# A delta-rule recurrence with a Fourier-mixing block: V's scaling, queries' products and one transposition moved in the order of work

## The chip, the cores and the metric

One core of one Trainium2 chip runs the whole kernel. The metric is the device time of one execution in microseconds (us); lower is better. Three runs of the kernel before took 741.8, 743.04 and 745.75 us, so their median is 743.04 us.

## The reference

Two blocks, one after the other. The first runs over 768 steps in order, for 4 batches and 8 heads with 48 values each:

```python
k_n = k / (np.linalg.norm(k, axis=-1, keepdims=True) + 1e-06)
for t in range(S):
    kt, vt, bt = (k_n[:, :, t], v[:, :, t], beta[:, :, t, None])
    y[:, :, t] = np.einsum('bhd,bhde->bhe', q[:, :, t], state)
    v_old = np.einsum('bhde,bhd->bhe', state, kt)
    state = state + bt[:, :, :, None] * np.einsum('bhd,bhe->bhde', kt, vt - v_old)
```

Each head keeps a 48 x 48 state. A step reads the state with the query and then corrects it with the key. The second block takes the 8 heads side by side as x (4 x 768 x 384):

```python
X = np.fft.fft(np.fft.fft(x, axis=1), axis=2)
u = x + np.real(X)
un = (u - mu) / np.sqrt(var + 1e-06)
return u + np.maximum(un @ w_ch1, 0.0) @ w_ch2
```

Here mu and var are the mean and variance of u over the last axis, and the hidden width is 1536. Everything is float32.

## The kernel before

**Tiles.** A batch of 768 steps is cut into 6 loads of 128 steps, and a load into 2 chunks of 64. Within a chunk, the dependence of steps on each other is a triangular 64 x 64 matrix for each head. Its inverse, applied to the keys and the values, turns 64 steps into a few matrix products. Four loads form a round, whose triangular blocks are inverted together on VectorE: 16 x 16 blocks in `invert16` (rounds 0 to 2), 32 x 32 blocks in `invert` (later rounds).

**One load.** Several generators make a load's parts; each `yield` is a point at which other work can be put between.

- `pre_a` transposes the keys (L320) and forms their Gram matrix on TensorE.
- `pre_q` transposes the queries (`turn`, PSUM to QT by ScalarE at L320), multiplies keys with queries (the product written `pair<-QT,KT` in the profile) and masks the result into LQ on VectorE (L555).
- `pre_m16` finishes the inverse of the 64 x 64 matrix from the 16 x 16 blocks. It takes a product with the part above the blocks (`one<-Z,GU`, copied to ND at L617) and then three more products, a short series: `MT,ND`, whose result is subtracted on VectorE (L645, into Z); `Z,ND`, copied by ScalarE into MT (L647); and `MT,ND` again, added on VectorE (L649, into MT). Then the values V are scaled by the keys' norms (L629, on VectorE for the first 8 loads and on GpSimd for later ones). At last, for batch 0, the load's last products `pair<-MT,K` and `one<-V,MT` give WT and U0.
- `step` does one chunk of the recurrence: a product with the state (`pair<-S,WT`), a subtraction from U on VectorE (L720), a product with the keys (`pair<-U,K`) and an addition into the next state S (L739). For later batches the forms are L698 (V less the product with the state) and L708 (U), and the first state of a batch is a copy (L737).
- `outputs` makes y: `pair<-S,QT` (copied to x at L762) and `pair<-U,LQ` (added to x at L772).

**The second block.** `folds` and `fourier` do the transform with tables; `mlp` normalises (un, L911), transposes on TensorE (the tile `ptr`, copied to unT at L922), and makes the products with w1 (tile `ph`, copied to hT at L936) and w2 (tile `po`). The weights arrive as 64-bit numbers and are converted by `weight`: ScalarE (L285, L277, L278) and VectorE (L286, L288, L292, L295, L299) share the work, with a ring of three or four loads E by DMA. A step's L285 waits until L292 of an earlier step has read the scratch tile that it writes.

**PSUM.** There are three rings with two tiles each: `pair`, `one` and `post` (ph, po and ptr). A new tile of a ring waits until the tile before the last one has been read.

**What sets the order.** Up to the middle of batch 0's second block, the order on TensorE, VectorE, ScalarE and GpSimd is written out by hand, as a list of `advance` and `drain` calls (`tc.manual_schedule(engines=engines)`). There the loop `for g in range(NL - 1)` works on load g's recurrence and, between its pieces, on the inverses of the next two loads: `nm` is the one of load g + 1 and `n2` the one of load g + 2. `fill` adds pieces of round 1's inversion, and `convert` pieces of the weights' conversion. `late` is the output of load g - 1. Then come the lines

```python
        done = 3 + KF
        inv = invert16(2)
    with tc.manual_schedule(engines={mybir.EngineType.PE}):
        drain(nq)
        for g in range(NL, NL + 2):
            period(g, side)
```

and for these two loads of batch 1 only TensorE's order is by hand; a scheduler places the others' instructions. Round 2's inversion begins here: its first piece clears M (L474) and transposes the Gram blocks into A (L475), and its next takes the square root of A's diagonal on ScalarE (nrm, L481), followed by a chain of small VectorE operations (L483 to L508) and 15 steps of a multiplication and an addition (L517, L520), with two more transpositions at the end (L523, L526).

Of the kernel before, what the change touches and what calls it, by code (L numbers as in the profile page):

```python
# [20 lines left out]
RL = 4  # L21
# [43 lines left out]
def kernel(  # L65
# [14 lines left out]
    NL = S // L  # L80
# [84 lines left out]
    def load_v(g, engine=None):  # L165
        if g < NLT:
            Vs[g] = wk.tile([128, 2, 4, D], F32, tag="V", bufs=2, name="V")
            halves(Vs[g], v, g, engine)
# [389 lines left out]
    def pre_m(g):  # L558

        r, li = divmod(g, RL)  # L560
        K, V = Ks[g % 3], Vs.pop(g)
        X = GXs[g // 2][:, li % 2]
# [5 lines left out]
                                op=ALU.mult)  # L568
        nc.gpsimd.tensor_tensor(V.rearrange("p c j d -> p (c j) d"),
                                V.rearrange("p c j d -> p (c j) d"),  # L570
# [27 lines left out]
    def pre_m16(g):  # L598


        r, li = divmod(g, RL)
        K, GU = Ks[g % 3], GXs.pop((g, 16))
        MTd, Md, nT = rounds[r]
        m8 = slice(8 * li, 8 * li + 8)
        tags = ("QT", "LQ") if g < 2 * RL else ("WT", "WT")
        Z = wk.tile([128, 8, 2, W], F32, tag=tags[0], bufs=2, name="Z")
        for e in range(2):
            nc.scalar.activation(Z[:, :, e, :], Md[:, m8, :], ACT.Copy, scale=m_blk[:, e:e + 1])
        if g != 2 * RL:
            yield  # L610
        px = ps_one()
        for m in range(8):
            for hh in range(2):
                mm(px[full[hh], C * m:C * m + C], GU[full[hh], m, :],
                   Z[full[hh], m].rearrange("p b t -> p (b t)"), m == 0)
        ND2 = wk.tile([128, 8, C], F32, tag=tags[1], bufs=2, name="ND")
        nc.scalar.activation(ND2.rearrange("p m t -> p (m t)"), px, ACT.Copy)  # L617
        MT = wk.tile([128, 8, 2, W], F32, tag="MT", bufs=2, name="MT")
        for e in range(2):
            if g == 0:  # L620
                nc.vector.tensor_scalar(MT[:, :, e, :], MTd[:, m8, :], m_blk[:, e:e + 1], None,
                                        op0=ALU.mult)
            else:
                nc.scalar.activation(MT[:, :, e, :], MTd[:, m8, :], ACT.Copy,  # L624
                                     scale=m_blk[:, e:e + 1])

        def scaled_v():
            V = Vs.pop(g)
            (nc.vector if g < 2 * RL else nc.gpsimd).tensor_tensor(  # L629
                V.rearrange("p c j d -> p (c j) d"), V.rearrange("p c j d -> p (c j) d"),  # L630
                nT[:, m8, None].broadcast_to([128, 8, D]), op=ALU.mult)
            return V

        V = None if g else scaled_v()
        flat = "p m b t -> p (m b t)"
        yield
        for i in range(3):
            pz = ps_one()
            src = Z if i == 1 else MT
            for m in range(8):  # L640
                for hh in range(2):
                    mm(pz[full[hh], C * m:C * m + C], ND2[full[hh], m, :],
                       src[full[hh], m].rearrange("p b t -> p (b t)"), m == 0)
            if i == 0:
                nc.vector.tensor_tensor(Z.rearrange(flat), MT.rearrange(flat), pz, op=ALU.subtract)  # L645
            elif i == 1:
                nc.scalar.activation(MT.rearrange(flat), pz, ACT.Copy)  # L647
            else:
                nc.vector.tensor_tensor(MT.rearrange(flat), Z.rearrange(flat), pz, op=ALU.add)  # L649
            if i < 2 or g < 2 * RL:  # L650
                yield
        V = V or scaled_v()
        if g >= NL:
            pre[g] = (K, MT, V)
            yield
            return
        yield
        WT = wk.tile([128, 2, 2, 2, C], F32, tag="WT", bufs=2, name="WT")
        U0 = wk.tile([128, 2, 4, D], F32, tag="U0", bufs=2, name="U0")
        pw = ps_pair()  # L660
        pu = ps_one()
        for c in range(2):
            for j in range(4):
                for hh in range(2):
                    mt = MT[full[hh], 4 * c + j].rearrange("p b t -> p (b t)")
                    jj, jp = divmod(j, 2)
                    o = (2 * c + jj) * C
                    mm(pw[full[jp], hh, o:o + C], K[full[hh], 4 * c + j, :], mt, c == 0 and jj == 0)
                    o = (4 * c + j) * D
                    mm(pu[full[hh], o:o + D], mt, V[full[hh], c, j, :], c == 0 and j == 0)  # L670
        nc.scalar.activation(U0.rearrange("p c j d -> p (c j d)"), pu[:, 0:8 * D], ACT.Copy)
        nc.scalar.activation(WT.rearrange("p h c j t -> p h (c j t)"), pw[:, :, 0:4 * C],
                             ACT.Copy)
        pre[g] = (K, WT)
        Us[g] = U0
        yield
# [291 lines left out]
    def advance(gen, n=1):  # L968
        for _ in range(n):
            if next(gen, "end") == "end":  # L970
                return False
        return True

    def drain(gen):
        for _ in gen:
            pass
# [121 lines left out]
    with tc.manual_schedule(engines=engines):  # L1098
# [4 lines left out]
        qs = [pre_q(g, QT6[:, g], LQ6[:, g]) for g in range(NL)]  # L1103
# [60 lines left out]
        def convert(n):  # L1164
            advance(conv, n)
# [9 lines left out]
        for g in range(NL - 1):  # L1175
            c0, c1 = step(g, 0), step(g, 1)
            nm, n2 = ms[g + 1], ms[g + 2]
            load_k(g + 2)
            load_v(g + 2)
            if g == 0:  # L1180
                advance(c0)
                fill(5)
                advance(nm)
                advance(n2)
                advance(c1)
                fill(5)
                advance(nm)
                advance(n2)
                advance(c1)
                fill(5)  # L1190
                advance(nm)
                advance(n2)
                drain(nm)
                advance(n2)
                drain(qs[1])
                advance(qs[2])
                advance(ms[3])
            else:
                advance(c0)
                if g == 2:  # L1200
                    advance(n2)
                else:
                    fill(5)
                if g > 2:
                    convert(1)
                advance(nm)
                advance(late)
                advance(c0)

                fill(5)  # L1210
                if g == 2:
                    convert(1)
                advance(n2)
                drain(late)
                if g == 4:
                    fold = folds(0)
                    fd = part(fold, 8)
                    advance(keys[0])
                advance(nm)
                advance(c1)  # L1220
                fill(4 if g == 1 else 3)
                if g > 1 and g != 4:
                    convert(2)
                drain(nm)
                advance(n2)
                advance(c1)
                if g == 4:
                    convert(2)
                    advance(n2)
                    drain(qs[g + 1])  # L1230
                    convert(1)
                else:
                    fill(1)
                    if g > 1:
                        convert(1)
                    advance(n2)
                    if g > 1:
                        convert(g - 1)
                    drain(qs[g + 1])
                if g + 2 < NL:  # L1240
                    advance(qs[g + 2])
                if g > 1 and g < 4:
                    advance(ms[g + 3])
            late = outputs(g)
            if g == 1:
                nc.sync.dma_start(out=evt, in_=cn["even"].ap())
                nc.sync.dma_start(out=odt, in_=cn["odd"].ap())
                nc.sync.dma_start(out=dtab, in_=cn["dtab"].ap())
            if g == 2:
                for i in range(2 * RL, 2 * RL + 3):  # L1250
                    load_c(i)
                load_q(NL)
                load_q(NL + 1)

        g = NL - 1
# [12 lines left out]
        late = outputs(g)  # L1268
# [4 lines left out]
        late = None  # L1273
# [36 lines left out]
            drain(m)  # L1310
        done = 3 + KF
        inv = invert16(2)
    with tc.manual_schedule(engines={mybir.EngineType.PE}):
        drain(nq)
        for g in range(NL, NL + 2):
            period(g, side)
# [48 lines left out]
```

## Time and profile before

| | us |
|---|---|
| median of three runs | 743.04 |
| the profiled execution | 743.66 |
| its span in the profile | 741.9 |
| TensorE busy in the span | 689.6 |
| VectorE busy | 377.1 |
| ScalarE busy | 262.5 |
| GpSimd busy | 79.1 |

The profiled execution took 0.62 us more than the median of the runs, and 1.76 us of it lie outside the span. In the time line, each row gives the start and the length in us, the engine, the line of the kernel, the operation, the written tile, the read tiles, the shape and the number of instructions. What stands in brackets is the idle time of the engine just before, and the instruction that ended it. In the table of stretches, each engine has its busy time and its number of instructions; the three numbers at the end are TensorE's granted clock as a share of the full clock, the DMA engines' share and GB/s.

The edited code covers these stretches of the span:

| stretch, us | what runs | TensorE busy, us |
|---|---|---|
| 50 to 115 | batch 0's recurrence, loads 0 to 5 | 52.6 of 65 |
| 115 to 160 | batch 0's transform and first products with w1 | 41.6 of 45 |
| 160 to 170 | between the first products and batch 1 | 5.3 of 10 |
| 170 to 200 | batch 1's first load, round 2's inversion | 28.6 of 30 |

### The profile page before, as it was taken

The numbers are of one execution on the slowest core, as the hardware profiler recorded it, in microseconds if no ns is written. First come the engines' busy times: TensorE is split into PE (matmuls) and PEld (weight loads), VectorE is DVE, ScalarE is ACT, GpSimd is POOL, SyncE is SP. The second block draws the span as 40 slices with busy tenths as digits, with TensorE's granted clock in tenths as the row PEclk, the third lists the DMA queues.
The fourth block names the chain that finished last, engine by engine and source line by source line (L and its number), as shares of the span: only waits on it lengthen the run. The fifth ranks groups of instructions, "written<-read, shape, count | busy, mean of one in ns | idle before, by whom it ended". The sixth has DMA issues, their size and how long they took to land.

```text
span 741.9 us, 23087 instructions
## 1 busy us (share of the span) xinstructions
PE 689.6 (93%) x10176; PEld 529.3 (71%) x10176; DVE 377.1 (51%) x957; ACT 262.5 (35%) x641; POOL 79.1 (11%) x138
## 2 busy tenths in 40 slices
PE   6878789969999978999999999999999999999998
PEld 5667777757667656878768778777677687777684
DVE  5877787798711996170596328288212241600000
ACT  4534774787324212234323243133223121221120
POOL 8000001110000102031101120030112100200000
PEclk8699999988999999999999999999999999999999
DMA  9842452153124211003212211001110000000000
GB/s 153 221 72 43 98 140 87 24 138 99 28 51 83 46 34 28 1 11 72 41 39 50 45 40 28 11 23 37 43 34 13 12 12 5 18 1 21 11 11 21
DMA packets 108791, 36.10 MB, mean 49 GB/s; under 512 B 101873, under 2 KB 105234, under 8 KB 108690
## 3 DMA queue, kind: packets, MB, share of 16 engines
q1 hardware_dynamic: 106866, 33.86, 21.1%
q8 instruction: 80, 1.31, 0.8%
q0 software_dynamic: 640, 0.43, 0.4%
q10 hardware_dynamic: 1184, 0.33, 0.3%
q14 instruction: 21, 0.17, 0.1%
HBM read 29.88 MB, written 4.72 MB: 47 GB/s over the span
## 4 chain that ended last, share of the span: by engine, by line
PE 75%; DVE 15%; ACT 6%; issue 2%; DMA 1%; DVEq 0%; ACTq 0%
PE po L110 24%; PE ph L110 21%; PE one L110 15%; PE pair L110 9%; PE one L113 2%; DVE M L450 1%; DVE tmp L446 1%; PE ptr L113 1%; PE unread L1111 1%; DVE tmp L517 1%; DVE M L520 1%; DMA C<-in_k_dram 1%; DVE Z L645 1%; DVE S L739 1%; DVE w L292 1%
## 5 line engine op out<-in xcount | busy, mean ns | idle before, releaser
L110 PE MATMUL po<-w,hT 128*128 128x384 f32 x576 | 204.8, 495 | 0.0
L110 PE MATMUL ph<-unT,w 128*128 128x256 f32 x828 | 197.2, 390 | 0.0
L110 PEld LDWEIGHTS ph<-unT,w 128*128 128x128 f32 x828 | 155.1, 193 | 23.2
L110 PEld LDWEIGHTS po<-w,hT 128*128 128x128 f32 x576 | 103.5, 190 | 56.4
L936 ACT ACTIVATE hT<-ph 128x256 f32<-128x256 f32 x138 | 52.8, 383 | 144.2 <-PE ph L110 143.3
L951 DVE TENSOR_TENSOR x<-x,po 128x384 f32<-128x384 f32 x24 | 13.2, 551 | 107.0 <-PE po L110 107.0
L739 DVE TENSOR_TENSOR S<-S,pair 128x192 f32<-128x192 f32 x40 | 14.0, 351 | 71.2 <-PE pair L110 71.1
L110 PEld LDWEIGHTS one<-V,MT 64*64 64x64 f32 x768 | 31.1, 143 | 20.0 <-issue 7.7
L882 DVE TENSOR_TENSOR x<-x,one 128x193 f32<-128x193 f32 x24 | 8.5, 355 | 66.5 <-ACT Q L873 66.5
L110 PE MATMUL one<-V,MT 64*64 64x48 f32 x768 | 36.4, 230 | 4.2 <-DVE V L698 2.6
L450 DVE TENSOR_TENSOR M<-M,tmp 128x31 f32<-128x31 f32 (+15 forms) x93 | 34.5, 371 | 3.2
L446 DVE TENSOR_TENSOR tmp<-A,M 128x31 f32<-128x31 f32 (+15 forms) x93 | 34.1, 366 | 2.5
L698 DVE TENSOR_TENSOR V<-V,pair 128x192 f32<-128x192 f32 x33 | 11.5, 349 | 37.6 <-PE pair L110 31.4
L110 PE MATMUL one<-MT,ND 64*64 64x64 f32 x768 | 28.9, 225 | 1.1 <-ACT MT L647 0.7
L110 PEld LDWEIGHTS one<-dtab,F 97*128 97x128 f32 (+1 forms) x192 | 25.1, 191 | 6.4 <-ACT KT L320 1.3
L894 POOL TENSOR_SCALAR rstd<-mv 128x1 f32<-128x1 f32 x24 | 6.6, 276 | 216.4 <-DVE mv L890 216.4
L110 PEld LDWEIGHTS one<-MT,ND 64*64 64x64 f32 x768 | 26.5, 141 | 2.3 <-ACT MT L624 1.1
L320 ACT ACTIVATE QT<-one 128x512 f32<-128x512 f32 x24 | 14.3, 595 | 38.7 <-PE one L113 38.6
L110 PE MATMUL one<-dtab,F 97*128 97x97 f32 (+1 forms) x192 | 26.0, 275 | 0.9 <-ACT KT L320 0.9
L566 POOL TENSOR_TENSOR MT<-A,pack 128x512 f32<-128x512 f32 x12 | 12.8, 1067 | 130.3 <-PE one L110 64.8
L110 PEld LDWEIGHTS pair<-U,K 64*64 64x64 f32 x704 | 15.5, 134 | 15.5 <-issue 13.2
L110 PEld LDWEIGHTS pair<-S,KT 48*64 48x64 f32 x528 | 10.7, 133 | 21.7 <-issue 10.9
(181 smaller groups left out, 1029.4 us busy)
## 6 DMA issues: line engine op xcount, KB each, us to landing
w<-in_moe_w_ch_dram SPq DMA_DIRECT2D x12, 384.0 KB, 7.2
E<-in_moe_w_ch_dram SPq DMA_DIRECT2D x12, 384.0 KB, 3.8
out_dram<-x SPq DMA_DIRECT2D x24, 192.0 KB, 1.9
K<-in_k_dram SPq DMA_DIRECT2D x92, 48.0 KB, 2.3
V<-in_v_dram SPq DMA_DIRECT2D x92, 48.0 KB, 2.3
C<-in_k_dram SPq DMA_DIRECT2D x18, 192.0 KB, 9.5
Q<-in_q_dram SPq DMA_DIRECT2D x18, 192.0 KB, 3.4
w<-in_q_dram SPq DMA_DIRECT2D x6, 192.0 KB, 7.9
```

The costliest lines, as they stand in the source:

```text
L110: nc.tensor.matmul(o, lhsT=lhsT, rhs=rhs, start=start, stop=stop, skip_group_check=True)
L113: nc.tensor.matmul(o, lhsT=src, rhs=ident[0:src.shape[0], 0:src.shape[0]], is_transpose=True, start=start, stop=True, skip_group_check=True)
L292: nc.vector.tensor_tensor(pieces[i - lag][1].rearrange("p c f -> p (c f)"), man0, num0.bitcast(F32), op=ALU.mult)
L320: nc.scalar.activation(dst.rearrange("p h j t -> p (h j t)"), pt, ACT.Copy)
L446: nc.vector.tensor_tensor(t, A[:, j + 1:W, j:j + 1].broadcast_to([128, n, j + 1]), M[:, j:j + 1, 0:j + 1].broadcast_to([128, n, j + 1]), o ...
L450: nc.vector.tensor_tensor(M[:, j + 1:W, 0:j + 1], M[:, j + 1:W, 0:j + 1], t, op=ALU.add)
L566: nc.gpsimd.tensor_tensor(MT, MTd[:, m8, None, :].broadcast_to([128, 8, 2, W]), m_blk[:, None, :, None].broadcast_to([128, 8, 2, W]), op=A ...
L698: nc.vector.tensor_tensor(R4, R4, pw[:, :, 0:2 * D].rearrange("p a (j e) -> p a j e", e=D), op=ALU.subtract)
L739: nc.vector.tensor_tensor(s1v, s0.rearrange("p h j e -> p h (j e)"), pk, op=ALU.add)
L882: nc.vector.tensor_tensor(near, near, pb[:, 0, 0:MH + 1], op=ALU.add)
L936: nc.scalar.activation(hT[:, fc, :], ph, ACT.Relu)
L951: nc.vector.tensor_tensor(x[:, T, :], x[:, T, :], po, op=ALU.add)
```

## The change

Three edits, all to the order of work; every instruction that ran before still runs.

1. In `pre_m16`, V is scaled in the same piece as the third product of the series, ahead of the addition at L649, for the first 8 loads. Before, it was a piece of its own after that addition (load 0 has its own place, which stays).
2. In the loop over batch 0's loads, the queries' products (`drain(qs[g + 1])`, and the next load's transposition `advance(qs[g + 2])`) come ahead of the second product of the series of load g + 2 rather than behind it. In the same loop `advance(late)` comes ahead of `advance(nm)`, so that a load's product `pair<-S,QT` stands ahead of the third product.
3. Round 2's inversion makes its first piece (M cleared, A transposed) at the end of the part whose order is all by hand, behind the first products with w1, rather than where the scheduler places it.

```diff
@@ pre_m16
                     mm(pz[full[hh], C * m:C * m + C], ND2[full[hh], m, :],
                        src[full[hh], m].rearrange("p b t -> p (b t)"), m == 0)
+            if i == 2 and V is None and g < 2 * RL:
+                V = scaled_v()
             if i == 0:
                 nc.vector.tensor_tensor(Z.rearrange(flat), MT.rearrange(flat), pz, op=ALU.subtract)
...
-        V = V or scaled_v()
+        if V is None:
+            V = scaled_v()
@@ loop over batch 0's loads
                 if g > 2:
                     convert(1)
+                advance(late)
                 advance(nm)
-                advance(late)
                 advance(c0)
...
                 if g == 4:
                     convert(2)
+                    drain(qs[g + 1])
                     advance(n2)
-                    drain(qs[g + 1])
                     convert(1)
                 else:
                     fill(1)
                     if g > 1:
                         convert(1)
+                    drain(qs[g + 1])
+                    advance(qs[g + 2])
                     advance(n2)
                     if g > 1:
                         convert(g - 1)
-                    drain(qs[g + 1])
-                if g + 2 < NL:
-                    advance(qs[g + 2])
@@ end of the part by hand
         done = 3 + KF
         inv = invert16(2)
+        advance(inv)
     with tc.manual_schedule(engines={mybir.EngineType.PE}):
```

## The prediction

> **What bounds the kernel now.** I read the page first, then the time lines of the matrix engine (PE), VectorE (DVE) and ScalarE (ACT) around the edited places, the chain of waits over the same stretches, and last PE's clock microsecond by microsecond.
>
> ```profile
> PE 689.6 (93%) x10176; PEld 529.3 (71%) x10176; DVE 377.1 (51%) x957; ACT 262.5 (35%) x641; POOL 79.1 (11%) x138
> ...
> PE   6878789969999978999999999999999999999998
> ...
> PEclk8699999988999999999999999999999999999999
> ```
>
> The 741.9 us are PE's nearly everywhere after slice 10 (185 us). All edited code lies before, in slices 2 to 10, where PE has holes. So the question is which wait ends each hole.
>
> ```profile
> 75.58 0.32 PE L110 MATMUL pair<-MT,K 64*64 64x64 f32 x2 [1.37 <-DVE x L772]
> 76.05 0.25 PE L110 MATMUL one<-V,MT 64*64 64x48 f32 x1
> ...
> 106.21 0.68 PE L110 MATMUL pair<-S,QT 48*64 48x48 f32 x32 [1.08 <-DVE LQ L555]
> ...
> 164.22 0.90 PE L113 MATMUL ptr<-pack,un 128*128 128x128 f32 x3 [4.11 <-ACT hT L936]
> ...
> 176.25 0.45 PE L110 MATMUL pair<-S,KT 48*64 48x48 f32 x16
> ...
> 180.25 0.67 PE L110 MATMUL one<-V,MT 64*64 64x48 f32 x16 [0.76 <-DVE V L698]
> ...
> 197.08 0.69 PE L110 MATMUL pair<-QT,KT 48*64 48x64 f32 x32 [0.67 <-DVE S L739]
> ```
>
> PE waits for DVE at the head of each load's last products (75.58, then again for the scaled values at 76.05), and loses 4.11 us at 160. At 197.08 PE and DVE meet: PE was free 0.67 us earlier.
>
> ```profile
> 69.93 0.64 DVE L555 TENSOR_TENSOR LQ<-pair,pack 128x512 f32<-128x512 f32 x1
> ...
> 75.45 0.55 DVE L629 TENSOR_TENSOR V<-V,nT 128x384 f32<-128x384 f32 x1
> ...
> 160.90 1.91 DVE L475 STREAM_TRANSPOSE A<-G 128x1024 f32<-128x1024 f32 x1
> ...
> 174.08 0.56 DVE L295 SCALAR_TENSOR_TENSOR O<-w,O 128x384 f32<-128x384 int32 x1 [1.45 <-ACT O L285]
> ...
> 175.75 0.35 DVE L737 COPY S<-pair 128x192 f32<-128x192 f32 x1
> ...
> 179.85 0.34 DVE L698 TENSOR_TENSOR V<-V,pair 128x192 f32<-128x192 f32 x1
> ```
>
> ```profile
> 162.84 0.26 ACT L481 ACTIVATE nrm<-A 128x32 f32<-128x32 f32 x1 [0.65 <-DVE A L475]
> ...
> 163.80 0.37 ACT L936 ACTIVATE hT<-ph 128x256 f32<-128x256 f32 x1
> ...
> 172.71 0.39 ACT L936 ACTIVATE hT<-ph 128x256 f32<-128x256 f32 x1 [1.80 <-PE ph L110]
> ```
>
> The hole at 160: DVE transposes A for 1.9 us, the weight conversion's L292 and ACT's L285 stand behind it, hT L936 behind that, and hT frees the PSUM tile that PE's transposes (ptr) need.
>
> ```profile
> 62.00:63.00 1.00, 0.27 (x10) 0.27 (x12) 0.94 (x3) 0.48 (x1) 0.00 (x0) 0.97 0.28 57
> ...
> 66.00:67.00 1.00, 1.00 (x40) 1.00 (x36) 0.00 (x0) 0.61 (x2) 0.00 (x0) 0.82 0.00 0
> ...
> 76.00:77.00 1.00, 0.95 (x38) 0.95 (x40) 0.97 (x3) 0.97 (x3) 0.00 (x0) 0.80 0.00 0
> ...
> 80.00:81.00 1.00, 0.37 (x16) 0.25 (x8) 0.74 (x2) 0.00 (x0) 0.00 (x0) 0.99 0.31 68
> ...
> 161.00:162.00 1.00, 0.00 (x0) 0.00 (x0) 1.00 (x1) 1.00 (x3) 0.00 (x0) 0.97 0.81 150
> ...
> 172.00:173.00 1.00, 1.00 (x27) 0.67 (x29) 0.63 (x3) 0.29 (x2) 0.00 (x0) 0.91 0.09 34
> ```
>
> The value after POOL's count is the granted clock. Between these lines it is 0.50: PE ran at half from 62.95 to 66.36, 76.60 to 80.01 and 161.94 to 172.17, the edges worked out from the mixed values.
>
> **What the Trainium skill says.** "TensorE: Matmul & The Clock Gate", Part 1, says that a window of 3413 ns which runs freely decides between half and full clock. The trace agrees: the six edges lie 3.41, 10.24, 3.41, 81.93 and 10.23 us apart, 1, 3, 1, 24 and 3 windows. Windows with about 2.0, 1.7 and 1.8 us of idle PE dropped the clock; windows with 1.4 and 1.5 us (35.65 to 39.06, 141.46 to 144.87) did not, so I take 1.6 us as the limit. As the phase is free, a hole of 2 us drops it in some executions only. Part 4 says that transposes don't count as busy for the gate; the window 165.35 to 168.76, busy 89% but partly with transposes, indeed did not restore the clock. The same page (Part 1, "Architectural detail") calls ACT and DVE strict FIFO queues; the nrm wait at 162.84, with hT behind it, agrees. These three carry the argument.
>
> **The change part by part.** Instruction orders are those of the changed program as built; no instruction is added or removed.
>
> *Values before the third sum (six loads).* Each V (0.47 us to the next instruction) moves ahead of L649. At the end of load 0, PE had V's operand late: its stream began at 53.44. Now V ends at 51.99, L649 at 52.67, and the stream starts at about 52.8: -0.6. At load 1 DVE is busy without a gap from 57.56 to 61.57 (U, fills, MT, S, fills), so V sits on the path of x L772, for which PE waits until 62.73: +0.47. Position after it -0.14. In later loads V fills a DVE gap and the second wait, 0.46 us at 75.58 to 76.05 and alike at 88.25 and 99.33, disappears.
>
> *Queries' products inside the series.* QT·KT (0.56) and the transposes (0.59) move ahead of Z·ND and fill PE's wait for Z L645, 0.72 at 67.88 and 81.10, 0.65 at 92.14. But S·QT now precedes the third product MT·ND, and its PSUM tile is one of two: it waits until LQ L555 has read its predecessor, as 106.21 shows. At load 1 to 2, LQ is late behind DVE's G transpose (67.91 to 70.0): S·QT can't start before 70.5, MT·ND ends at 72.2 instead of 71.35, S and A's transpose come 0.7 later, and PE resumes at 76.15 or so: nothing left of the gain, position +0.1. At load 2 to 3: Z·ND 81.55, S·QT 83.4 (LQ ends 83.35), MT·ND ends 85.15, ACT's Z is ready at 85.3 rather than 85.77, x L772 at 87.2, the stream at 87.85 against 88.71: -0.85, position -0.75. Load 3 to 4 repeats it, but L292's wait for ACT takes most: -0.2 more. Load 4 to 5 is bound by LQ as before. Sum of the recurrence: -0.95.
>
> *The two later loads.* V for load 6 now stands before L649 at 114.09; the fold's last step would end at 118.8 instead of 118.3 and PE wants it at 118.70: +0.1. V for load 7 stands before L649 at 144.63; from there DVE to L286 (147.39) and ACT L277 (147.78, idle 1.71) is the chain of waits: +0.47. V's old places (129.02, 148.71) gate nobody.
>
> *A's transposition.* It now stands after four more conversion steps; nrm L481 stands on ACT behind two hT copies. With the old clock: mv 161.0, L292 ends 161.5, ACT L285 at 162.1, hT 162.55, ptr at 162.95: 1.27 earlier. But 2.84 us of hole stay, above the limit in all but a tenth of phases, so PE resumes at half clock. At half: second transposes 164.4, V·MT 165.3, ph products 166.3 to 171.35, two hT (the second at 171.4, a few tenths less if the gate opens early; I take 170.9), then L277, L285, L278 (1.75), L481 at 172.65, and DVE's L483 only at 172.95. DVE had A transposed by 170.75 and stands idle 1.7 us behind L483. Before, the conversion's L295 waited there instead, and S needed only 1.7 us of DVE afterwards. Now seventeen instructions (L483 to L500, 4.2 us by their spacings) stand ahead of S: S at 177.2 against 175.75, V L698 at 181.45 against 179.85. PE, done with its ph products at 174.5, waits for S about 2.7 us: a hole that the old order doesn't have, above the limit, so the next 2.86 us of ph products run at half (5.1): V·MT at 182.9 against 180.25. From there PE ran 16.16 us without a hole to 196.41, hence 199.06 against 197.08: +2.0. If the second drop stays out, V sets it: 181.85 + 16.16 = 198.0, +0.9. If the gate never closes at 162, DVE has no wait at all: its 2.0 us of idle go, -1.8. If both phases fall late: hT at 171.4, V·MT at 183.5, and a late reopening, +3.3. DVE's own end (196.84) would be +0.4 to +1.1: not the bound. Nothing after 200 has slack that returns or swallows this: PE is busy for 523.1 of the last 541.9 us (689.6 less 166.5 up to there), and the later inversions start from PE.
>
> *Queues.* SP gets the beta loads a little earlier, POOL's memset of M moves behind the last GU memset, far from use at 178.9. Weight loads E follow DVE's L299, 3.8 us to landing, due 0.5 us or more ahead of L285. Taken as nothing; a late E would cost up to 0.5.
>
> Sum: -0.95 + 0.1 + 0.47 + 2.0 = +1.6 us. Against the profiled execution, 743.66 (span 741.9 and 1.76 around it), that is 745.3. It lies 0.6 above the median of 743.04, so the forecast is 743.04 + 1.6 = **744.6**. The measurement can tell about 0.5%, 3.7 us, from no change; the forecast lies within.
>
> **The rivals.**
> - *The gate stays open.* 162.95 falls so that no window has 1.6 us of hole, or it opens again before the ph products: DVE's waits vanish. -0.95 + 0.57 - 1.8 = -2.2: 740.9; with one of the two earlier slow phases also gone (1.7 each), 739.2. For it: the hole is 1.27 shorter. Against: 2.84 is still well above the limit.
> - *The clock drops everywhere (the slower side).* One mechanism: PE's holes, at 60.1 (1.98 before, 2.45 now) and at 174.5 (none before, 2.7 now), each cross the limit; half clock doubles what follows up to the end of the next full window. It decides from 1.6 us of hole in one window. Recurrence -0.95 + 1.7, later loads 0.57, late phases 3.3: +4.6, 747.7. For it: three drops in the trace after like holes. Against: the phase must be unlucky twice.
> - *The transposition only changes places.* DVE's stalls before and after L483 balance, stage 160 to 197 is even: -0.4, 742.7. For it: DVE's work there is the same. Against: S stands behind more of it.
>
> **How the numbers follow.** Forecast 0.45, gate open 0.25, drops 0.20, even 0.10. Faster by over 0.5% is four tenths of the second and a little of others: 0.12. Slower: seven tenths of the third and a tenth of the first: 0.19. Within: 0.69. The unknown costs of the forecast itself (0.9 to 3.3 for the last stage, half a microsecond either way in the recurrence) give 743 to 746.5; for 8 in 10 the range takes in the rivals' centres: 740.3 to 747.9.
>
> **What would show it.** In the new profile: no second wait for V at the products of loads 2 to 5; S·QT waiting for LQ after load 1, ending near 0.8 us; the hole at 160 down to about 2.8; nrm's L483 on DVE waiting 1 to 2 us for ACT; PE waiting for S 2 to 3 us where S·KT stood at 176.25. I am wrong if that hole is absent, or if PE reaches the QT·KT of 197.08 earlier than before.

## The result, and the profile after

The changed kernel took 743.62 us (median of 20 runs, 741.05 to 748.66), the kernel before 744.4 us beside it (20 runs, 741.53 to 746.21). The ratio is 0.9993 with a 95% interval from 0.9975 to 1.0011, so no difference shows. Its profiled execution took 744.35 us, with a span of 742.6.

Three lines of its page stand below: busy time by engine, then TensorE's (PE's) busy share and its granted clock in 40 slices.

```profile
PE 689.8 (93%) x10176; PEld 529.9 (71%) x10176; DVE 377.5 (51%) x957; ACT 262.7 (35%) x641; POOL 79.5 (11%) x138
...
PE   6877989977999978999999999999999999999998
...
PEclk9799989999999997999999999999999999999999
```

Busy times are the same within 0.6 us, as the edits move work and add none. But the clock's row has its low slices elsewhere: before, slices 1, 9 and 10 stood at 8 and slice 2 at 6; now slices 2 and 16 stand at 7, slice 6 at 8. Hence a comparison of two spans says little here. I compare stretches between points that both kernels have:

| stretch | before | after | change | forecast |
|---|---|---|---|---|
| start to the first state's copy S (no edit has acted) | 45.18 | 43.82 | -1.36 | 0 |
| M1: that S to load 5's first sum Z | 57.28 | 56.39 | -0.89 | -0.95 |
| M2: that Z to the hole at 160 us | 57.65 | 59.41 | +1.76 | +0.57 |
| M3: the hole's start to the QT·KT near 197 us | 36.97 | 36.45 | -0.52 | +2.0 |
| from there to the end of the span | 544.82 | 546.53 | +1.71 | 0 |
| span | 741.9 | 742.6 | +0.7 | +1.6 |

The ends of M1 on VectorE (DVE), before:

```profile
45.18 0.35 DVE L737 COPY S<-pair 128x192 f32<-128x192 f32 x1
...
102.46 0.69 DVE L645 TENSOR_TENSOR Z<-MT,one 128x512 f32<-128x512 f32 x1 [0.97 <-ACT WT L672]
```

and after:

```profile
43.82 0.35 DVE L740 COPY S<-pair 128x192 f32<-128x192 f32 x1
...
100.21 0.69 DVE L647 TENSOR_TENSOR Z<-MT,one 128x512 f32<-128x512 f32 x1 [0.54 <-ACT WT L675]
```

No edit reaches the first and the last row, and they go with the clock: ahead of 45 us PE ran 10.2 us at half clock, where it was 20.5 before, and behind 197 us it ran 10.2 us at half clock, where it was 3.4. The clock acts inside M1, M2 and M3 as well, so these changes aren't the edits' alone. The time line of PE around the edits:

```profile
68.92 0.68 PE L110 MATMUL pair<-S,QT 48*64 48x48 f32 x32 [1.10 <-DVE LQ L555]
74.62 0.28 PE L110 MATMUL pair<-MT,K 64*64 64x64 f32 x2 [2.23 <-DVE x L775]
...
162.43 0.55 PE L113 MATMUL ptr<-pack,un 128*128 128x128 f32 x3 [2.82 <-ACT hT L939]
...
175.60 0.45 PE L110 MATMUL pair<-S,KT 48*64 48x48 f32 x16 [2.91 <-DVE S L740]
179.71 0.67 PE L110 MATMUL one<-V,MT 64*64 64x48 f32 x16 [0.88 <-DVE V L701]
...
196.07 0.69 PE L110 MATMUL pair<-QT,KT 48*64 48x64 f32 x32 [0.21 <-DVE S L742]
```

(Lines below 644 keep their numbers, those behind V's new place are 2 or 3 higher.) S·QT now waits for LQ at 68.92. The hole at 160 has shrunk from 4.11 to 2.82 us, and a new wait for S, 2.91 us, stands at 175.60, where before PE didn't wait. VectorE and ScalarE in that stretch:

```profile
168.24 1.96 DVE L475 STREAM_TRANSPOSE A<-G 128x1024 f32<-128x1024 f32 x1
...
171.11 0.18 DVE L483 TENSOR_SCALAR nrm<-nrm 128x32 f32<-128x32 f32 x1 [0.47 <-ACT nrm L481]
...
175.19 0.35 DVE L740 COPY S<-pair 128x192 f32<-128x192 f32 x1
...
179.31 0.35 DVE L701 TENSOR_TENSOR V<-V,pair 128x192 f32<-128x192 f32 x1
```

```profile
169.08 0.38 ACT L939 ACTIVATE hT<-ph 128x256 f32<-128x256 f32 x1 [0.91 <-PE ph L110]
169.87 0.56 ACT L285 ACTIVATE O<-E 128x384 f32<-128x384 uint32 x1
170.83 0.25 ACT L481 ACTIVATE nrm<-A 128x32 f32<-128x32 f32 x1
```

A's transposition comes 7.3 us later than before, and the square root L481 stands on ScalarE behind hT and L285. VectorE waits 0.47 us for it. And the clock, in the table of stretches (PE's granted share is the number before the last two):

```profile
104.00:105.00 1.00, 0.88 (x48) 0.76 (x48) 1.00 (x4) 1.00 (x3) 0.00 (x0) 1.00 0.05 5
105.00:106.00 1.00, 0.81 (x44) 0.69 (x37) 0.97 (x5) 0.27 (x1) 0.00 (x0) 0.80 0.48 88
...
163.00:164.00 1.00, 0.44 (x2) 0.44 (x3) 1.00 (x4) 0.98 (x2) 0.09 (x1) 0.82 0.72 151
164.00:165.00 1.00, 1.00 (x14) 0.67 (x15) 1.00 (x4) 0.55 (x3) 0.00 (x0) 0.50 0.68 259
...
167.00:168.00 1.00, 1.00 (x6) 0.89 (x5) 1.00 (x4) 1.00 (x3) 0.00 (x0) 0.98 0.71 280
...
174.00:175.00 1.00, 0.00 (x0) 0.00 (x0) 1.00 (x5) 0.68 (x2) 0.00 (x0) 1.00 0.60 227
```

The clock fell at 163.61 as forecast, but came back at 167.02, after one window of 3.41 us; before it stayed at half for three. The second hole, with PE idle through 174 to 175, didn't lower it. And it fell at 105.60, where before it held.

### The profile page after: what moved, and what is told of

It reads as the page before. It is cut to its first block, busy times and chain, and to the rows that moved or that the text cites. A ratio compares the mean times of both kernels' runs of the same rounds, so it can differ in the third digit from the quotient of the medians.

```text
span 742.6 us, 23085 instructions
## 1 busy us (share of the span) xinstructions
PE 689.8 (93%) x10176; PEld 529.9 (71%) x10176; DVE 377.5 (51%) x957; ACT 262.7 (35%) x641; POOL 79.5 (11%) x138
## 4 chain that ended last, share of the span: by engine, by line
PE 73%; DVE 17%; ACT 6%; issue 2%; DMA 1%; DVEq 0%; ACTq 0%
PE po L110 24%; PE ph L110 21%; PE one L110 15%; PE pair L110 9%; PE one L113 2%; DVE M L450 1%; DVE tmp L446 1%; PE ptr L113 1%; PE unread L1114 1%; DVE M L520 1%; DVE tmp L517 1%; ACT GU L395 1%; DMA C<-in_k_dram 1%; DVE w L292 1%; ACT G L385 1%
## 5 line engine op out<-in xcount | busy, mean ns | idle before, releaser
L450 DVE TENSOR_TENSOR M<-M,tmp 128x31 f32<-128x31 f32 (+15 forms) x93 | 34.5, 371 | 3.2
L446 DVE TENSOR_TENSOR tmp<-A,M 128x31 f32<-128x31 f32 (+15 forms) x93 | 34.1, 367 | 2.5
```

What stands on the lines that cost most here:

```text
L446: nc.vector.tensor_tensor(t, A[:, j + 1:W, j:j + 1].broadcast_to([128, n, j + 1]), M[:, j:j + 1, 0:j + 1].broadcast_to([128, n, j + 1]), o ...
L450: nc.vector.tensor_tensor(M[:, j + 1:W, 0:j + 1], M[:, j + 1:W, 0:j + 1], t, op=ALU.add)
```

## The experiments

The theory from the result: the edits' own gains and losses are each below 1 us; what decides a run is in how many windows (stretches of 3.41 us, at whose edges the clock changes) the holes left around them let the clock fall. The rivals: the edits' parts cancel exactly (then each alone moves the time), or VectorE's queue sets the stretches whatever PE's clock is.

All were timed in five rounds beside the kernel before (medians of that between 743.38 and 745.84 us). M1, M2 and M3 are those of the table above, from one profile each; "half" is the time at half clock in the whole span, and the last column counts the windows at half clock that lie in M1, M2 and M3.

| kernel | median | ratio | 95% interval | M1 | M2 | M3 | half | windows |
|---|---|---|---|---|---|---|---|---|
| before | | 1 | | 57.28 | 57.65 | 36.97 | 41.0 | 2, 0, 3 |
| after | 743.62 | 0.9993 | 0.9975 to 1.0011 | 56.39 | 59.41 | 36.45 | 37.6 | 2, 2, 1 |
| e1_values | 743.48 | 0.9999 | 0.9981 to 1.0016 | 55.98 | 59.87 | 33.58 | 30.7 | 1, 1, 1 |
| e2_order | 742.31 | 0.9990 | 0.9976 to 1.0004 | 57.61 | 60.13 | 35.49 | 37.5 | 2, 3, 2 |
| e3_transp | 745.0 | 1.0010 | 0.9992 to 1.0027 | 58.91 | 59.63 | 36.47 | 34.1 | 2, 2, 1 |
| e4_s_on_act | 746.3 | 1.0033 | 1.0014 to 1.0052 | 56.42 | 59.43 | 37.86 | 41.0 | 2, 2, 2 |
| e5_before_warm | 741.62 | 0.9970 | 0.9953 to 0.9988 | 57.21 | 60.67 | 34.92 | 27.3 | 0, 4, 0 |
| e6_after_warm | 747.98 | 1.0047 | 1.0032 to 1.0062 | 56.78 | 59.31 | 38.43 | 35.5 | 0, 2, 0 |
| e7_pool292 | 749.68 | 1.0067 | 1.0040 to 1.0094 | 56.38 | 59.76 | 41.91 | 47.8 | 2, 2, 4 |
| e8_mended | 742.1 | 0.9980 | 0.9961 to 0.9999 | 55.47 | 57.63 | 39.69 | 37.5 | 2, 0, 4 |
| e9_before_fill | 742.09 | 0.9970 | 0.9954 to 0.9986 | 56.90 | 58.95 | 35.96 | 27.3 | 0, 0, 1 |
| e10_mend12_fill | 739.04 | 0.9939 | 0.9918 to 0.9961 | 52.95 | 58.95 | 36.46 | 27.3 | 0, 1, 1 |
| e11_mend_fill | 741.68 | 0.9963 | 0.9946 to 0.9981 | 53.08 | 58.80 | 37.45 | 30.7 | 0, 0, 2 |
| e12_mend12_fill8 | 737.65 | 0.9912 | 0.9887 to 0.9936 | 52.85 | 58.35 | 34.95 | 30.7 | 0, 1, 0 |

A stretch of one profile scatters by more than the edits' gains. No edit reaches M1 in e3_transp, and it is 58.91 us against 57.28 before, with the same two windows at half clock; 0.99 us of it is a stop of PE that nothing in the profile ends. The changed kernel, e4_s_on_act and e7_pool292, which have the same recurrence, agree within 0.04 us.

The mean clock of every run is on record, and from it and the span follows the run's time at half clock. Over the changed kernel's 20 runs the time rises with it (correlation 0.80), over the 67 runs of the kernel before beside e1 to e4 less so (0.54), over the 22 runs of e2_order not at all (-0.34). So the clock is a large part of the difference between runs, but not all of it.

### Each edit alone

e1_values has the change's first edit only, e2_order the second, e3_transp the third (their lines are in the diff above).

e1_values:

> The kernel before with the first edit alone (V scaled ahead of the third sum). My theory: the recurrence, measured from the first state's copy S (45.18 before) to load 5's first sum Z (102.46), takes 57.28 us before and 57.28 - 0.6 (load 1's values ready) + 0.47 (load 2's V on VectorE's full stretch) - 3 x 0.46 (second waits gone at loads 3 to 5) = 55.8 us here, if the clock drops in the same places. From there to the hole at 160: 57.65 before, +0.57 here. Median about 0.9 us under before. Rival, that V's place is worth nothing since PE waits for x at the same points anyway: 57.3 and an even median.

e2_order:

> The kernel before with the second edit alone (queries' products and S-QT ahead). My theory: it is no gain by itself. At load 2 S-QT waits about 0.8 us for LQ, which stands behind VectorE's transposition of G, and the third product is about 0.7 us late; the later loads give 0.3 to 0.6 back. First state to load 5's Z: 57.3 to 57.7 us against 57.28; median within 0.5 us of before. Rival, that filling PE's wait for Z (0.65 to 0.72 at three loads) is the gain of the change: 55.3 us and a median 2 us lower.

e3_transp:

> The kernel before with the third edit alone (A transposed behind the first products). My theory: PE's hole at 160 shrinks from 4.1 to 2.8 us, and a new wait for S of 2 to 3 us appears where S-KT stood at 176.25; from the start of the hole to the product QT-KT at 197.08 it takes 36.97 us before and 36.3 to 39 here, by how far the half clock reaches; median within 1.5 us of before. Rival, that the 1.3 us stay gained to the end: 35.7 us, median 1.3 lower, whatever the clock does.

None of the three differs measurably from before, so gains and losses of several microseconds that cancel are ruled out. e2_order's M1 is 57.61, as expected, and its M3 fell to 35.49 without an edit there: two windows at half clock, where before had three. e1_values's M1 of 55.98 is near the expected 55.8 by luck: that assumed two windows at half clock, and there was one. So its M1 doesn't measure the first edit. Its M2 of 59.87 holds a window at half clock (154.5 to 158.0 us) that before doesn't have. e3_transp has the two marks of the third edit, a wait of 2.83 us for hT and of 2.90 us for S, and an M3 of 36.47, as in the changed kernel: the new hole belongs to that edit. e1_values has a surprise. One line of its time line of VectorE:

```profile
158.63 1.97 DVE L475 STREAM_TRANSPOSE A<-G 128x1024 f32<-128x1024 f32 x1
```

No edit of its own touches A's transposition, yet the scheduler now put it 2.3 us earlier than before (160.90), ahead of the statistics and the conversion. PE's wait in the hole was 2.53 us, no wait for S followed, and M3 was 33.58 us, the shortest of all, with one window at half clock in it. That is the opposite direction to the third edit.

### Taking the new wait away

e4_s_on_act lets ScalarE copy the first state of batch 1:

```diff
-            if begin:
+            if begin and b == 1:
+                nc.scalar.activation(s1v, pk, ACT.Copy)
+            elif begin:
                 nc.vector.tensor_copy(s1v, pk)
```

> The changed kernel with batch 1's first state copied by ScalarE instead of VectorE, so that the wait for S in the changed kernel's profile (2.91 us at 175.60) goes. If VectorE's sum of work sets the meeting point (my theory by now: there PE waits 0.21 us for VectorE's S at 196.07), the stretch from the start of the hole at 160 to QT-KT stays at 36.0 to 36.5 us (36.45 in the changed kernel) and the median within 0.5 us of the changed kernel's. Rival, that the wait for S is a loss on the path, as my prediction had it: 33.6 us and 2 to 3 us off the median.

The wait for S went, and a longer one for V came in its place, in PE's time line:

```profile
162.99 0.55 PE L113 MATMUL ptr<-pack,un 128*128 128x128 f32 x3 [2.84 <-ACT hT L941]
...
180.13 0.67 PE L110 MATMUL one<-V,MT 64*64 64x48 f32 x16 [3.71 <-DVE V L701]
```

V stands in the same VectorE queue behind the same chain, and a further window at half clock (181 to 185) followed. M3 was 37.86 us, so neither expectation came true. The copy of S alone is not the cost; PE now waits for V, which stands behind the same work on VectorE.

e7_pool292 gives twelve of VectorE's conversion steps (L292 of the second weights) to GpSimd:

```diff
-                nc.vector.tensor_tensor(pieces[i - lag][1]...
+                (nc.gpsimd if last else nc.vector).tensor_tensor(pieces[i - lag][1]...
```

> The changed kernel with the second weights' conversion multiplied on GpSimd instead of VectorE (12 instructions of 0.47 us less on VectorE between 140 and 190 us). Theory 'VectorE's queue sets the meeting at 160-197 us': the wait for the first state's copy (2.9 us) falls below 1 us, M3 from 36.45 to 33-35 us, whole 740-742 us. Rival 'TensorE's own work sets it': M3 within 0.7 us of 36.45, the idle time only goes elsewhere. Rival 'GpSimd is too slow': the second weights' hh products wait, M3 38 or more.

The third case, that GpSimd is too slow, came true. GpSimd's time line:

```profile
163.85 3.02 POOL L292 TENSOR_TENSOR w<-O 128x384 f32<-128x384 f32 x3
```

A step that takes 0.55 us on VectorE takes about 1.1 us there, VectorE waits 1.57 us for one at 164.88, and hT comes later: the hole grew to 4.83 us, and 13.6 us at half clock followed between 164 and 186. VectorE wasn't relieved either: its own steps beside GpSimd's became longer, as L288 at 165.94 with 2.06 us rather than 0.35. So the run doesn't tell whether less work on VectorE alone would help.

### Taking the losses back

e8_mended keeps the early V for loads 1, 3, 4 and 5, and at load 2 the old order of two lines:

```diff
-            if i == 2 and V is None and g < 2 * RL:
+            if i == 2 and V is None and g in (1, 3, 4, 5):
@@
-                advance(late)
-                advance(nm)
+                if g == 2:
+                    advance(nm)
+                    advance(late)
+                else:
+                    advance(late)
+                    advance(nm)
```

> The changed kernel with the parts taken back that my reading prices as losses: V of loads 2, 6 and 7 is again scaled after the third product, and at load 2 the third inversion's step stands again ahead of the late outputs. My reading: Z of load 5 0.7-1.2 us earlier than in the changed kernel from the same start (M1 55.2-55.7 at the same count of half-clock stretches), and 0.5 us less ahead of 160 us; whole 741.5-742.5 us. Rival 'these losses are covered by the clock's windows': M1 within 0.4 us of 56.4, time within 0.7 us of the changed kernel's 743.6.

M1 is 55.47, 0.92 us below the changed kernel's, as expected, with the same two windows at half clock in it; one profile's scatter, above, is larger than that. M2 is 57.63, that of before. But M3 is 39.69. PE's time line and the table of stretches show why:

```profile
174.49 0.68 PE L110 MATMUL pair<-S,KT 48*64 48x48 f32 x16 [2.91 <-DVE S L740]
```

```profile
174.00:175.00 1.00, 0.51 (x16) 0.51 (x16) 1.00 (x5) 0.44 (x1) 0.00 (x0) 0.54 0.42 55
175.00:176.00 1.00, 1.00 (x10) 0.82 (x4) 1.00 (x6) 0.17 (x1) 0.00 (x0) 0.50 0.82 289
...
181.00:182.00 1.00, 1.00 (x15) 0.89 (x12) 1.00 (x4) 0.97 (x3) 0.00 (x0) 1.00 0.01 2
```

The wait for S is 2.91 us long, as in the changed kernel, but here it fell so that one window held about 2.5 us of it, and PE ran at half clock from 174.1 to 180.9. From S·KT to QT·KT it took 22.38 us, 1.91 more than in the changed kernel (175.60 to 196.07). The other 1.33 us of M3 lie ahead of S·KT, where the first hole cost two windows at half clock instead of one: PE's wait of 0.58 us between the two halves of un fell into the first of them, and the clock didn't come back at its end. Holes of the same length cost one window in the changed kernel and four here, by where the windows' edges lie.

### Filling the holes

In the next kernels, products whose results nothing reads stand on PE where it would wait. `warm` is new; the calls differ in their counts:

```diff
+    def warm(n, ring, src):
+        unread = ring()
+        unread = unread[:, 0, :] if len(unread.shape) == 3 else unread
+        for _ in range(n):
+            nc.tensor.matmul(unread[:, 0:DM], lhsT=src[:, 0:128], rhs=src, start=True, ...)
@@ in period, behind its first pieces
+            if g == NL and i == 0:
+                warm(8, ps_pair, evt[:, 0, 0:DM])
@@ in the loop, ahead of drain(nm)
+                if g < 3:
+                    warm(5 if g == 1 else 4, ps_one, zeros)
```

e5_before_warm is the kernel before with these:

> The kernel before, with extra TensorE products whose results nothing reads: 8 in the hole at 160 us ahead of A's second transposition, 5 and 4 in the pauses of the recurrence of loads 1 and 2. Theory 'clock gate': the half-clock stretches of before at 63, 76 and 162 us go (17 us of half clock become 0), M1 (first state's copy to load 5's first sum Z) falls from 57.3 to 54-56 us, M3 (hole at 160 to QT.KT near 197) from 37.0 to 33-35 us, and the whole is 738-741 us against 743.4. Rival 'VectorE and ScalarE set these stages': the clock is full there, but M1 and M3 stay within 0.7 us of 57.3 and 37.0, time even. Rival 'the fill costs': the products delay their followers, M1 58 or more.

e6_after_warm is the changed kernel with 6 at 160 us, 7 ahead of S·KT, 6 and 4 in the loop:

> The changed kernel with such unread products in its holes: 6 at 160 us, 7 at 172 us (while TensorE waits for the first state's copy), 6 and 4 in the recurrence of loads 1 and 2. Theory 'clock gate': half clock at 61-65, 75-78 and 164-167 us goes, M1 from 56.4 to 53-55 us, M3 from 36.45 to 34-35.5 us (VectorE's queue then ends the stage: wait for S or V of 3-4 us), whole 738-741 us. If the change's earlier V and queries' products are of use only under a full clock, it is below e5_before_warm by 0.5 us or more; if they only change places, within 0.5 us of it. Rival 'VectorE sets it': M1 and M3 within 0.7 us of the changed kernel's, time even.

In both, the half clock at 62, 76 and 162 us went. In e5_before_warm M3 fell by 2.05 us. M1 didn't fall. Each product took 0.70 us, so five took 3.49 us in a hole that was 1.98 us long, and the fill ate most of what the first window gave. At load 4's first sum Z the kernel was still 1.38 us ahead of before; it lost 1.30 of that in the last load, where PE stood for 1.09 us at 100.52 although nothing in the profile holds it. Then the clock fell at 102.08 for four windows, which is in M2. In e6_after_warm seven products ahead of S·KT did worse: S was ready at 176.3, S·KT began at 179.42. Its M3 of 38.43 without any half clock is the price of the fill, and says nothing on the edits; the whole is 0.5% slower than before.

e9_before_fill has 5 products at 160, 2 and 2 in the loop and one each in two small holes near 100 us:

```diff
                 if g == 4:
+                    warm(1, ps_one, evt[:, 0, 0:DM])
                     convert(2)
@@ last load
         fill(2)
+        warm(1, ps_one, evt[:, 0, 0:DM])
         advance(late)
```

> The kernel before with fewer unread products, fitted to the holes by the 0.70 us that each took in e5_before_warm: 5 at 160 us (hole of 4.1), 2 and 2 in the recurrence (holes of 2.0 and 1.4), 1 and 1 near 100 and 103. Theory 'the fill of e5_before_warm ate what the full clock gave': M1 53.5-55.5 against 57.3, M3 33-34.5, no half clock in 102-116; whole 738-740.5. Rival 'VectorE and ScalarE set M1 in any case': M1 56.5-57.5, M3 34.5-35, whole 741-742.

e10_mend12_fill adds the first two edits as in e8_mended, without the third:

> As e9_before_fill, with V early at loads 1, 3, 4, 5 and the queries' products of the change, the late outputs of load 2 as before, and no early transposition. If the two parts are worth 1.5-2 us under a full clock as worked out from the chain (V at load 1 0.14, S.QT's waits for LQ 0.85, load 0's V left out): M1 1.0-1.7 us below e9_before_fill's. Rival 'they only change places with other waits': M1 within 0.4 us of e9_before_fill's.

e11_mend_fill adds the third as well, with 3 products at 160:

> As e10_mend12_fill, with the early transposition and 3 unread products at 160 us (hole of 2.8). Theory 'the transposition only changes places': a wait of 2-3 us for the first state's copy, M3 within 0.7 us of e10_mend12_fill's 33-34.5, whole even with it. If its 1.3 us counts once the clock is full: M3 0.8-1.3 us lower. Rival 'the second hole drops the clock': half clock near 174-181 as in e8_mended, M3 36 or more.

With the loop's holes filled to their size, load 4's first sum Z came 43.33 us after the first S in e9_before_fill, against 46.13 before: 2.8 us where before had two windows at half clock. From there e9_before_fill lost it again, as its PE time line shows:

```profile
92.79 0.74 PE L110 MATMUL one<-MT,ND 64*64 64x64 f32 x18 [1.13 <-issue]
97.22 0.32 PE L110 MATMUL pair<-U,LQ 64*64 64x48 f32 x5 [1.56 <-issue]
...
102.92 0.27 PE L110 MATMUL pair<-U,K 64*64 64x48 f32 x5 [1.58 <-issue]
```

These stops lie in the middle of rows of like products and nothing that the profile shows ends them; before had 0.50 us of them between 85 and 105 us. The first two lie in M1, the third behind it, in M2. So e9_before_fill's M1 of 56.90 is no measure of the edits. Its M3 of 35.96 missed the expected 33 to 34.5, as the clock fell at 168.01. At load 4's Z, e10_mend12_fill stands at 42.34, 0.99 us ahead of e9_before_fill: the low end of what I expected of the two edits. (e9_before_fill also has a stop of 0.85 us at 52.82, at the products that V held up, and e10_mend12_fill hasn't.) Of the 3.95 us between their M1, the rest lies between the two last sums, where the stops are. By the whole time, 0.9939 (0.9918 to 0.9961) against 0.9970 (0.9954 to 0.9986), the two edits can't be told from nothing, as the intervals overlap.

e11_mend_fill against e10_mend12_fill: the third edit brought a wait of 3.87 us for S, and the clock fell for two windows:

```profile
171.29 0.68 PE L110 MATMUL pair<-S,KT 48*64 48x48 f32 x16 [3.87 <-DVE S L740]
```

```profile
170.00:171.00 1.00, 0.00 (x0) 0.00 (x0) 1.00 (x6) 0.97 (x2) 0.00 (x0) 0.52 0.21 83
171.00:176.00 5.00, 4.71 (x26) 3.81 (x27) 5.00 (x19) 1.18 (x3) 0.00 (x0) 0.50 0.24 83
```

So the expectation "second hole drops the clock" holds, M3 37.45. In e10_mend12_fill the clock fell too, at 163, since 5 products left 0.95 us of wait between the two halves of un, and more around it. e12_mend12_fill8 has 8 there and is otherwise the same:

> As e10_mend12_fill, with 8 unread products at 160 us instead of 5, so that they also cover the 0.95 us for which TensorE waits for the second half. Theory 'the clock's drop at 163 us comes from what is still idle between the halves': no half clock in 160-172, M3 34.5-35.5 us against 36.5, M1 52.5-53.5 as in e10_mend12_fill, whole 737-739 us. Rival 'three more products cost what the clock gives': M3 36-37 us, time even with e10_mend12_fill's 739.0.

```profile
155.58 5.43 PE L1020 MATMUL pair<-evt 128*128 128x384 f32 x16 [0.62 <-ACT GU L395]
161.60 0.55 PE L113 MATMUL ptr<-pack,un 128*128 128x128 f32 x3 [0.27 <-ACT hT L939]
173.10 0.67 PE L110 MATMUL one<-V,MT 64*64 64x48 f32 x16 [0.44 <-DVE V L701]
189.92 0.69 PE L110 MATMUL pair<-QT,KT 48*64 48x64 f32 x32 [0.67 <-DVE S L742]
```

PE's time line of e12_mend12_fill8 shows the fill of 5.43 us where the hole was (the profile has two instructions for each of the 8 products), and no wait ahead of S·KT. M3 is 34.95 us without any half clock, as expected. The whole took 737.65 us, ratio 0.9912 (0.9887 to 0.9936). That interval, from six runs, lies wholly below the changed kernel's. This version, with two edits mended, the third left out and the holes filled, has the lowest median of all; e10_mend12_fill's interval overlaps it.

## Why the prediction was right, point by point

No change was forecast and none showed. The +1.6 us within it did not: the ratio's interval allows -1.9 to +0.8 us. Over M1, M2 and M3 the profiles differ by +0.35 us, and that this is small is partly luck: a term of +1.24 that the prediction didn't have and one of +2.0 that came as -0.52 nearly make up for each other.

One of the prediction's two signs of being wrong came true by its letter: PE reached the QT·KT at 196.07, earlier than 197.08. Of that, 1.36 us arose before any edit acts; from the first state's copy on it is 0.35 us later.

- **Recurrence, -0.95.** It measured -0.89. Load 0's gain was 0.60 us (forecast 0.6), and at load 1's end the position was -0.13 (forecast -0.14). S·QT's wait for LQ was 1.10 us rather than 0.8. Load 3's first sum stood at -0.02, load 4's at -0.33, load 5's at -0.89, so the gain came one load later than forecast, and its sum held. e8_mended fits the mechanism, as taking back what the prediction priced as losses there, load 2's V and order, gave 0.92 us. It isn't shown by the number, since the M1 of two kernels with the old recurrence, 57.28 and 58.91, lie further apart than that.
- **Load 7's V, +0.47.** From the key products at 142.49 to the fold's at 153.86, 11.37 us against 10.85: +0.52. ScalarE's wait for L286 grew from 1.71 to 2.23 us. Load 6's +0.1 can't be told from the half clock around it.
- **Between them, a term that was missing.** M2 grew by 1.76 us; load 7 explains 0.52. The rest, 1.24 us, goes with PE's half clock from 105.6 to 112.4, which the prediction did not foresee; e8_mended, without it and with V late, has M2 at 57.63.
- **A's transposition, +2.0.** The steps came as written: ptr's wait 2.82 us (forecast 2.84), L483 waits for ScalarE, S stands behind L500 and PE waits 2.91 us for it (forecast 2.7). The term that was mis-sized is the clock. The prediction let PE run at half until the ph products ended at 171.35; the half clock ended at 167.02, behind a window in which PE was busy throughout. So the second hT came at 169.08, not 170.9, VectorE waited 0.47 us, not 1.7, and S was copied at 175.19, not 177.2. Then "above the limit, so the next 2.86 us of ph products run at half" failed: the second hole left the clock alone. V·MT came at 179.71, not 182.9. M3 measured -0.52 us, but with one window at half clock against three before; e2_order, in the old order with two, took 35.49 us, less than the changed kernel. In e8_mended and e11_mend_fill the second drop did come; from S·KT to QT·KT they took 22.38 and 22.03 us, against 20.47.
- **"The transposition only changes places"**, forecast as the least likely case at 742.7, is nearest to what the profile shows for that stretch, and e3_transp alone (1.0010, 0.9992 to 1.0027) fits it, though that interval reaches +2.0 us as well. What speaks against the edit all the same is that no kernel with it had an M3 below 36.4 us, while the two without it whose hole is filled to its end have 34.92 and 34.95.
- **The limit of 1.6 us** was read wrongly. The window of before from 73.19 to 76.60, taken as about 1.7 us, held 1.51 us of idle PE and lost the clock; the one from 141.46, with 1.47, kept it. The last section has more windows.

Still open: what an earlier transposition, as e1_values had it, would bring by itself, since no run isolates it.

## What to carry to other kernels

Where PE's clock follows windows that run freely, a moved instruction that saves half a microsecond can cost or win three by the windows that the remaining holes fall into (M3 was 36.45 us with one window and 39.69 with four); compare stretches between common points with their time at half clock, not spans. Size a fill of unread products by the hole it is to cover, between the first idle moment and the last wait: too few left the drop, too many cost more than the clock. An instruction that is put back in a queue delays what waits behind its chain. An earlier place may be better, as e1_values's M3 suggests; no run isolates it.

## What was unexpected in the hardware

- Idle time in a window doesn't decide alone whether the clock falls. The windows follow from the edges of the half clock. In the 14 profiles, between 40 and 205 us, all 25 windows at full clock with 1.82 us of idle PE or more were followed by half clock, and none with less than 1.08. Between these, 15 lost the clock and 45 kept it. In the changed kernel the window from 173.85 to 177.26 held 1.75 us and kept it; the window from 102.18 to 105.59, with 1.30 us among products of 48 and 64 rows, lost it. Small tiles don't explain this, as the window from 37.34 to 40.75, with 1.51 us among products of 64 rows, kept it. What decides there stays open. The Trainium skill ("TensorE: Matmul & The Clock Gate", Part 1, "What's actually happening") names at least one idle window of about 3.4 us as the condition for half clock; here 39 of 40 such drops came without a window that was idle throughout (e7_pool292's at 164.87 is the other), so the measurement decides.
- The clock comes back only behind a window that PE fills almost wholly. Of the 57 windows at half clock in the same stretch, all 37 with at most 0.11 us of idle PE were followed by full clock, and none of the 17 with 0.27 us or more. So a wait of half a microsecond, harmless at full clock, prolongs the half clock: 0.48 us in the window from 105.61 of the changed kernel did. One later window of that kernel, from 286.5 us, stayed at half without any idle time; why is open.
- The same page's Part 4 says that transposes don't count as busy in the same way, and the prediction leaned on it. The window from 163.61 to 167.02 of the changed kernel restored full clock although some 0.8 us of it were transposes. Before, the window that failed had 0.36 us of idle besides, and in e2_order a window with 0.39 us and no transposes failed too (106.07 to 109.48). So the transposes alone do not keep the clock down.
- PE stopped for 1.13, 1.56 and 1.58 us inside rows of like products in e9_before_fill, and for about 1 us in e3_transp and e5_before_warm. The cause is not shown.
- In e7_pool292 a VectorE step took about as long as the GpSimd multiplication that ran beside it, whatever its own size: at 172.38 L288 took 1.16 us (0.35 in the changed kernel), at 187.15 L518, on 78 elements for each partition, 1.03 us (0.24 there). GpSimd's multiplications at 172.32 and 186.96 took 1.00 and 1.13 us.
